# A gated feed-forward layer on one core: two x loads on one queue, gate pieces held on ScalarE, the first crossbar load in two

## The chip, the core and the metric

The kernel runs on one core of a Trainium2 chip. The core has TensorE (matrix multiply, "PE" in the profile; its weight loads are "PEld"), VectorE ("DVE"), ScalarE ("ACT"), GpSimd ("POOL") and SyncE ("SP"). [...] SyncE, ScalarE and GpSimd issue the DMA transfers between HBM and the on-chip memory. The metric is the device time of one launch in microseconds (us); lower is better. Before the change it is 163.2 us, the median of three runs (163.05 to 163.49).

## The reference

For 2048 rows of x with 640 columns the layer computes, in bf16:

```python
B, S, D, F = 1, 2048, 640, 1536

def reference(x, w_gate, w_up, w_down):
    g = _silu(x @ w_gate)
    u = x @ w_up
    return (g * u) @ w_down
```

`w_gate` and `w_up` are 640 x 1536, `w_down` is 1536 x 640.

## The kernel before, in words

The 2048 rows are worked in four blocks of 512 (`S_BLK`, the variable `sb`). The 640 columns of x are five slices of 128 (`KD`, `kd`), the 1536 columns in the middle twelve slices of 128 (`KF`, `fc`). A matmul contracts over the partitions, so x is needed turned: `xT` holds, for each `kd`, 128 features on the partitions and the rows along the free dimension. For each block and each `fc`, `proj` (line 197) makes five matmuls of `w_gate` into a psum buffer `pg` and five of `w_up` into `pu`; `gate` (line 212) takes silu of `pg` on ScalarE and multiplies it with `pu` on VectorE into `aT`. After the twelve `fc` of a block, `aT` is multiplied with `w_down` (lines 274 and 303) and stored. VectorE works out the last four rows of x separately by dot products (line 148) beside this.

Blocks 1 to 3 of x come through the crossbar: `turn_x` (line 108) issues a DMA that transposes on the way (line 110). The first block comes in two ways. Its first two chunks of 128 rows (`PE_X = 2`) are loaded plainly into `x_sb` (line 86), turned by TensorE with an identity matrix (line 190, five transposes for each chunk), and copied out of psum by ScalarE (`kd` 0 and 1) and VectorE (`kd` 2 to 4, line 195). Its last two chunks, the "late half", come through the crossbar.

The first loads and their queues stand in lines 112 to 122. x chunk 0 is on SyncE and x chunk 1 on ScalarE. The gate weights of the first two `fc` are cut at `kd` = 2 (`K_CUT`): pieces 0 and 1 on SyncE, pieces 2 to 4 on ScalarE. Those of the up weights: pieces 0 and 1 on GpSimd, 2 to 4 on SyncE. Then SyncE issues the crossbar's load for the late half, and after that the remaining weights in three larger chunks (line 83), `w_down` and the rest. ScalarE runs one small silu (line 122) so that its function table is loaded before it is needed. GpSimd builds the identity matrix with two instructions, a write of zeros and a select (`make_identity`, line 71).

`head` (line 221) writes out the order of the first two `fc` of the first block. TensorE begins with `N_WARM` small matmuls that compute nothing that is used (the fillers, line 177), then the ten transposes, then the gate matmuls of the early half (line 240: for `kd` 0 and 1 on 128 columns at a time, for `kd` 2 to 4 on 256), then the up matmuls of the early half, and then the late half: gate, up and `gate()` of `fc` 0, then the same for `fc` 1. `keep_order` fixes the order in which the instructions of TensorE, ScalarE and GpSimd were written; at the end of the body it does so for VectorE and SyncE. `issue_order` fixes the order of two instructions without a wait. The psum buffers `pg` and `pu` share four places, so that a later `fc` can only start when ScalarE or VectorE has read the buffer that it takes over.

Of the kernel before, what the change touches and what calls it, by code (L numbers as in the profile page):

```python
# [10 lines left out]
def _body(  # L11
# [8 lines left out]
    nc = tc.nc  # L20
# [3 lines left out]
    ACT = mybir.ActivationFunctionType  # L24
# [8 lines left out]
    KD = D // P  # L33
    KF = F // P
    S_BLK = 512
    NSB = S // S_BLK
    SUB = S_BLK // P
    DA = 512
    Q = 32
    N_WARM = 20  # L40
    T = 4
    WT_STEP = 4
    PE_X = 2
    K_CUT = 2
    ROW_J = 0
    W_CHUNKS = [(0, 2), (2, 4), (4, 8), (8, 12)]
    assert D % P == 0 and F % P == 0 and S % S_BLK == 0 and D > DA and SUB == 4
# [8 lines left out]
    ident = consts.tile([P, P], bf16)  # L56
    x_sb = consts.tile([P, PE_X, D], bf16)
    xT = consts.tile([P, KD, S], bf16)
    wg_sb = consts.tile([P, KD, F], bf16)
    wu_sb = consts.tile([P, KD, F], bf16)  # L60
# [7 lines left out]
    row_s = consts.tile([P, KF, T], f32)  # L68
    prod = consts.tile([P, D], f32)

    make_identity(nc, ident[:])

    x_v = x2.rearrange("(c p) d -> p c d", p=P)
    xt_v = x2.rearrange("s (kd p) -> s kd p", p=P)
    wg_v = w_gate.rearrange("(kd p) f -> p kd f", p=P)
    wu_v = w_up.rearrange("(kd p) f -> p kd f", p=P)
    wd_v = w_down.rearrange("(kf p) d -> p kf d", p=P)

    def wslice(a, b):
        return slice(a * P, b * P)  # L80
# [4 lines left out]
    def load_x(eng, c0, c1):  # L85
        eng.dma_start(out=x_sb[:, c0:c1, :], in_=x_v[:, c0:c1, :])

    def issue_order(a, b):
        tc.add_manual_dep(
            b,  # L90
            a.name,
            mybir.DependencyInfo(
                mybir.DependencyClass.NoSync, mybir.DependencyReason.DATA
            ),
            reason="issue_order",
        )

    def keep_order(engine):

        traced = [i for i in nc.cur_bb.bb.instructions if i.engine == engine]  # L100
        for a, b in zip(traced, traced[1:]):
            issue_order(a, b)

    ones = consts.tile([P, 1], bf16)
    silu_first = consts.tile([P, 1], f32)
    nc.vector.memset(ones[:], 1.0)  # L106

    def turn_x(c0, c1):
        s_sl = slice(c0 * P, c1 * P)
        nc.sync.dma_start_transpose(out=xT[:, :, s_sl], in_=xt_v[s_sl])  # L110

    load_x(nc.sync, 0, 1)
    load_x(nc.scalar, 1, 2)
    f_sl = wslice(*W_CHUNKS[0])
    for dst, src, first, second in (
        (wg_sb, wg_v, nc.sync, nc.scalar),
        (wu_sb, wu_v, nc.gpsimd, nc.sync),
    ):
        for eng, k_sl in ((first, slice(0, K_CUT)), (second, slice(K_CUT, KD))):
            eng.dma_start(out=dst[:, k_sl, f_sl], in_=src[:, k_sl, f_sl])  # L120
    turn_x(PE_X, SUB)
    nc.scalar.activation(silu_first[:], ones[:, 0:1], ACT.Silu)
    for a, b in W_CHUNKS[1:]:
        load_w(nc.sync, wg_sb, wg_v, a, b)
        load_w(nc.sync, wu_sb, wu_v, a, b)
# [4 lines left out]
    def turn_w(dst, src):  # L130
        for a in range(0, KF, WT_STEP):
            nc.sync.dma_start_transpose(
                out=dst[:, a : a + WT_STEP, :], in_=src[:, a : a + WT_STEP, :]
            )

    turn_x(1 * SUB, 2 * SUB)
    nc.sync.dma_start(
        out=x_row[:],
        in_=x2[S - T : S, :].rearrange("t d -> (t d)").partition_broadcast(P),
# [19 lines left out]
    def row_tail():  # L159
        for _ in dots:  # L160
            pass
        nc.scalar.activation(row_s[:], row_g[:], ACT.Silu)
        nc.vector.tensor_tensor(
            out=aT[:, :, S - T : S], in0=row_s[:], in1=row_u[:], op=ALU.mult
        )
# [3 lines left out]
    def do_dots(n):  # L169
        for _ in range(n):  # L170
            next(dots, None)
# [3 lines left out]
    def warm(n):  # L175
        for _ in range(n):
            nc.tensor.matmul(  # L177
                pw[:, 0:P],
                lhsT=ones[:].broadcast_to([P, P]),
                rhs=ones[:].broadcast_to([P, P]),  # L180
                start=True,
                stop=True,
            )

    def transpose_chunk(c, parts):
        c_sl = slice(c * P, (c + 1) * P)
        for copy, tag, k0, k1 in parts:
            pt = psum.tile([P, k1 - k0, P], bf16, tag=tag, name="pt")
            for kd in range(k0, k1):
                nc.tensor.transpose(  # L190
                    out=pt[:, kd - k0, :],
                    in_=x_sb[:, c, kd * P : (kd + 1) * P],
                    identity=ident[:],
                )
            copy(out=xT[:, k0:k1, c_sl], in_=pt[:])  # L195

    def proj(ps, w_sb, fc, sb, c0, c1):
        for kd in range(KD):
            nc.tensor.matmul(  # L199
                ps[:, c0:c1],  # L200
                lhsT=w_sb[:, kd, fc * P : (fc + 1) * P],
                rhs=xT[:, kd, sb * S_BLK + c0 : sb * S_BLK + c1],
                start=(kd == 0),
                stop=(kd == KD - 1),
            )

    def gu_tiles():
        pg = psum.tile([P, S_BLK], f32, tag="gu", name="pg", bufs=4)
        pu = psum.tile([P, S_BLK], f32, tag="gu", name="pu", bufs=4)
        return pg, pu  # L210

    def gate(pg, pu, sb, fc, n_s):

        s0 = sb * S_BLK
        sg = work.tile([P, S_BLK], f32, name="sg")
        nc.scalar.activation(sg[:, 0:n_s], pg[:, 0:n_s], ACT.Silu)  # L216
        nc.vector.tensor_tensor(  # L217
            out=aT[:, fc, s0 : s0 + n_s], in0=sg[:, 0:n_s], in1=pu[:, 0:n_s], op=ALU.mult
        )

    def head():

        dve, act = nc.vector.tensor_copy, nc.scalar.copy
        split = [(act, "po_a", 0, 2), (dve, "po_b", 2, KD)]
        late = PE_X * P
        (pg0, pu0), (pg1, pu1) = gu_tiles(), gu_tiles()  # L230
        warm(N_WARM)
        transpose_chunk(0, split)
        transpose_chunk(1, split)
        early = [(kd, c * P, (c + 1) * P) for c in range(PE_X) for kd in range(K_CUT)]
        early += [(kd, 0, late) for kd in range(K_CUT, KD)]
        for kd, c0, c1 in early:
            for fc, pg in ((0, pg0), (1, pg1)):


                nc.tensor.matmul(  # L240
                    pg[:, c0:c1],
                    lhsT=wg_sb[:, kd, wslice(fc, fc + 1)],
                    rhs=xT[:, kd, c0:c1],
                    start=(kd == 0 and c0 == 0),
                    stop=(kd == KD - 1),
                )
        proj(pu0, wu_sb, 0, 0, 0, late)
        proj(pu1, wu_sb, 1, 0, 0, late)
        for fc, pg, pu in ((0, pg0, pu0), (1, pg1, pu1)):
            proj(pg, wg_sb, fc, 0, late, S_BLK)  # L250
            proj(pu, wu_sb, fc, 0, late, S_BLK)
            gate(pg, pu, 0, fc, S_BLK)
        keep_order(mybir.EngineType.PE)
        keep_order(mybir.EngineType.Activation)
        keep_order(mybir.EngineType.Pool)

    head()
    for sb in range(NSB):
        n_s = S_BLK if sb < NSB - 1 else S_BLK - T
        for fc in range(KF):  # L260
            if sb == 0 and fc < 2:
                continue
            pg, pu = gu_tiles()
# [22 lines left out]
        for q in range(P // Q):  # L286
            nc.scalar.dma_start(
                out=out2[
                    sb * S_BLK : sb * S_BLK + n_t, DA + q * Q : DA + (q + 1) * Q
                ].rearrange("(i r) c -> r i c", r=Q),  # L290
                in_=ot_q[q * Q : (q + 1) * Q, :].rearrange("r (i c) -> r i c", c=Q),
            )

        for j in range(SUB):
# [5 lines left out]
            for c0, c1, tag in cols:  # L300
# [10 lines left out]
                if c1 < D:  # L311
                    nc.scalar.copy(ot[:], po[:])  # L312
                    eng = nc.sync
                else:
                    nc.vector.tensor_copy(out=ot[:], in_=po[:])  # L315
                    eng = nc.sync
                if 0 < j and not last:
                    do_dots(3)
                if sb == NSB - 1 and j == ROW_J:
                    row_tail()  # L320
                eng.dma_start(out=out2[s0 : s0 + P, c0:c1], in_=ot[:])
        if sb == 0:
            turn_x(2 * SUB, 3 * SUB)
            turn_w(wuT, wut_v)
            turn_x(3 * SUB, 4 * SUB)
# [72 lines left out]
def kernel(tc, *args):  # L398
    _body(tc, *args)
    tc.close()  # L400
    tc.compile()
    _trim(tc.nc)
# [30 lines left out]
```

## Time and profile before

| what | value |
|---|---|
| median of three runs | 163.2 us (163.05 to 163.49) |
| the profiled execution | 163.61 us, span 162.2 us |
| TensorE busy | 159.8 us, 98% of the span |
| VectorE busy | 110.8 us, 68% |
| ScalarE busy | 42.9 us, 26% |
| GpSimd busy | 1.5 us, 1% |
| DMA moved | 15.86 MB, mean 98 GB/s |

The span runs from the first to the last instruction of the profiled execution; its own time is 1.4 us longer. Busy time counts matmuls whose ends are modelled, so a busy TensorE is not a TensorE at its peak. The chain of waits follows the work that ended last back to the start, at each step to what released it; its shares say which engine or transfer the end hung on. A DMA's row on its issuer's queue shows the time in which the transfer is issued; the time from issue to landing is listed apart.

### The profile page before, as it was taken

Reading aid. Unit: us, or ns where it says so; the run is one execution under the profiler, and the core shown is the slowest. Engines: PE = TensorE matmul, PEld = TensorE weight load, DVE = VectorE, ACT = ScalarE, POOL = GpSimd, SP = SyncE. Lnnn points to the kernel's source line nnn. Section 1 sums busy time; section 2 is a strip of 40 time slices with the busy share of each in tenths; the row PEclk is TensorE's granted clock in tenths of the full one; section 3 lists DMA queues with packets and bytes.
Section 4 is the critical chain, followed back from the end, with each engine's and each line's share of the span. In section 5 each row is a group of like instructions: output and inputs, shape, how many; then the busy total and the mean of one; then the engine's idle time right before and its main releaser. Section 6 shows DMA issues by size and latency. Waiting matters only on the chain.

```text
span 162.2 us, 2119 instructions
## 1 busy us (share of the span) xinstructions
PE 159.8 (98%) x798; PEld 78.1 (48%) x798; DVE 110.8 (68%) x249; ACT 42.9 (26%) x74; POOL 1.5 (1%) x7
## 2 busy tenths in 40 slices
PE   8999999999999999999999999999999999999995
PEld 8854444444444444444444444444444444445454
DVE  1042233599469999979919999979964999993000
ACT  5132222112222222221222322221214222222121
POOL 3000000000000000000000000000000000000000
PEclk9999999999999999999999999999999999999999
DMA  7999999993179996003110000000320000000212
GB/s 215 275 343 350 363 217 220 240 216 87 35 164 161 205 177 136 4 0 34 65 65 0 0 4 2 0 0 1 63 68 33 0 0 0 0 0 4 50 39 73
DMA packets 42217, 15.86 MB, mean 98 GB/s; under 512 B 33216, under 2 KB 42048, under 8 KB 42208
## 3 DMA queue, kind: packets, MB, share of 16 engines
q1 hardware_dynamic: 33680, 14.75, 37.6%
q10 hardware_dynamic: 8480, 0.85, 3.4%
q8 instruction: 6, 0.10, 0.3%
q0 software_dynamic: 48, 0.13, 0.2%
q14 instruction: 3, 0.02, 0.1%
HBM read 6.88 MB, written 2.62 MB: 59 GB/s over the span
## 4 chain that ended last, share of the span: by engine, by line
PE 97%; DMA 2%; DVE 0%; issue 0%
PE pu L199 32%; PE pg L199 31%; PE po_a L303 26%; PE po_t L274 6%; DMA x_sb<-in_x_dram 2%; PE pg L240 1%; PE pt L190 1%; DVE ot_b L315 0%
## 5 line engine op out<-in xcount | busy, mean ns | idle before, releaser
L199 PE MATMUL pu<-xT,wu_sb 128*128 128x512 bf16 (+2 forms) x250 | 59.7, 370 | 0.0
L199 PE MATMUL pg<-xT,wg_sb 128*128 128x512 bf16 (+2 forms) x240 | 58.5, 374 | 0.0
L217 DVE TENSOR_TENSOR aT<-sg,pu 128x512 bf16<-128x512 f32 (+1 forms) x48 | 32.8, 684 | 32.4 <-PE pu L199 28.1
L216 ACT ACTIVATE sg<-pg 128x512 f32<-128x512 f32 (+1 forms) x48 | 28.6, 597 | 70.8 <-PE pg L199 66.2
L303 PE MATMUL po_a<-wd_sb,aT 128*128 128x512 bf16 (+2 forms) x216 | 42.8, 358 | 0.0
L148 DVE SCALAR_TENSOR_TENSOR prod<-wgT,x_row 128x640 f32<-128x640 bf16 x48 | 39.4, 821 | 1.1
L148 DVE SCALAR_TENSOR_TENSOR prod<-wuT,x_row 128x640 f32<-128x640 bf16 x48 | 39.4, 822 | 1.0
L199 PEld LDWEIGHTS <-wu_sb 128*128 128x128 bf16 x250 | 24.5, 98 | 27.3
L199 PEld LDWEIGHTS <-wg_sb 128*128 128x128 bf16 x240 | 23.5, 98 | 26.9
L303 PEld LDWEIGHTS <-aT 128*128 128x128 bf16 x216 | 20.7, 98 | 21.6
L312 ACT CAST ot<-po_a 128x512 bf16<-128x512 f32 (+1 forms) x17 | 9.5, 561 | 32.0 <-PE po_a L303 20.9
L274 PE MATMUL po_t<-aT,wd_sb 128*128 128x512 bf16 (+1 forms) x48 | 10.4, 366 | 0.0
L274 PEld LDWEIGHTS <-wd_sb 128*128 128x128 bf16 x48 | 4.7, 98 | 5.1
L315 DVE CAST ot_b<-po_a 128x128 bf16<-128x128 f32 x1 | 0.3, 292 | 9.9 <-PE po_a L303 9.9
L283 ACT CAST ot_t<-po_t 128x512 bf16<-128x512 f32 (+1 forms) x4 | 2.2, 559 | 11.6 <-PE po_t L274 11.6
L148 DVE DVE_READ_ACCUMULATOR prod<-wuT,x_row 128x1 f32 x48 | 4.0, 83 | 0.0
L148 DVE DVE_READ_ACCUMULATOR prod<-wgT,x_row 128x1 f32 x48 | 3.9, 82 | 0.0
L285 DVE STREAM_TRANSPOSE ot_q<-ot_t 128x512 bf16<-128x512 bf16 (+1 forms) x4 | 2.7, 678 | 1.7 <-ACT ot_t L283 1.7
L195 DVE COPY xT<-pt 128x384 bf16<-128x384 bf16 x2 | 0.7, 358 | 3.5 <-PE pt L190 3.5
L177 PE MATMUL pw<-ones 128*128 128x128 bf16 x20 | 2.3, 310 | 0.3 <-DVE ones L106 0.3
L240 PE MATMUL pg<-xT,wg_sb 128*128 128x128 bf16 (+1 forms) x14 | 2.2, 347 | 0.0
L177 PEld LDWEIGHTS <-ones 128*128 128x128 bf16 x20 | 2.0, 144 | 0.3 <-DVE ones L106 0.3
(16 smaller groups left out, 8.4 us busy)
## 6 DMA issues: line engine op xcount, KB each, us to landing
wd_sb<-in_w_down_dram SPq DMA_DIRECT2D x1, 1920.0 KB, 14.0
out_dram<-ot SPq DMA_DIRECT2D x15, 128.0 KB, 1.7
wg_sb<-in_w_gate_dram SPq DMA_DIRECT2D x2, 640.0 KB, 8.2
wu_sb<-in_w_up_dram SPq DMA_DIRECT2D x2, 640.0 KB, 8.8
x_row<-in_x_dram SPq DMA_DIRECT2D x1, 640.0 KB, 5.2
out_dram<-ot_q ACTq DMA_DIRECT2D x12, 32.0 KB, 1.9
wg_sb<-in_w_gate_dram SPq DMA_DIRECT2D x1, 320.0 KB, 4.4
wu_sb<-in_w_up_dram SPq DMA_DIRECT2D x1, 320.0 KB, 4.9
```

What stands on the lines that cost most here:

```text
L148: nc.vector.scalar_tensor_tensor(out=prod[:], in0=wT[:, fc, :], scalar=1.0, in1=x_row[:, t, :], op0=ALU.mult, op1=ALU.mult, accum_out=acc[ ...
L177: nc.tensor.matmul(pw[:, 0:P], lhsT=ones[:].broadcast_to([P, P]), rhs=ones[:].broadcast_to([P, P]), start=True, stop=True,)
L190: nc.tensor.transpose(out=pt[:, kd - k0, :], in_=x_sb[:, c, kd * P : (kd + 1) * P], identity=ident[:],)
L199: nc.tensor.matmul(ps[:, c0:c1], lhsT=w_sb[:, kd, fc * P : (fc + 1) * P], rhs=xT[:, kd, sb * S_BLK + c0 : sb * S_BLK + c1], start=(kd == 0 ...
L216: nc.scalar.activation(sg[:, 0:n_s], pg[:, 0:n_s], ACT.Silu)
L217: nc.vector.tensor_tensor(out=aT[:, fc, s0 : s0 + n_s], in0=sg[:, 0:n_s], in1=pu[:, 0:n_s], op=ALU.mult)
L240: nc.tensor.matmul(pg[:, c0:c1], lhsT=wg_sb[:, kd, wslice(fc, fc + 1)], rhs=xT[:, kd, c0:c1], start=(kd == 0 and c0 == 0), stop=(kd == KD ...
L274: nc.tensor.matmul(po_t[:], lhsT=wd_sb[:, kf, DA:D], rhs=aT[:, kf, sb * S_BLK : sb * S_BLK + n_t], start=(kf == 0), stop=(kf == KF - 1),)
L283: nc.scalar.copy(ot_t[:], po_t[:])
L285: nc.vector.transpose(out=ot_q[:], in_=ot_t[:])
L303: nc.tensor.matmul(po[:], lhsT=aT[:, kf, s0 : s0 + P], rhs=wd_sb[:, kf, c0:c1], start=(kf == 0), stop=(kf == KF - 1),)
L312: nc.scalar.copy(ot[:], po[:])
```

## The change

Both x chunks are loaded by SyncE. ScalarE first loads its function table with the small silu and then issues the gate pieces 0 and 1 and piece 2 of the up weights. The gate pieces write into `wg_sb`, into which GpSimd now writes one column (`wg_sb[:, 0, 0:1]`) between the two instructions of the identity matrix; so that transfer waits for this write. SyncE issues gate pieces 2 to 4 and up pieces 3 and 4. The identity's write of zeros is written out and `make_identity` is told to leave it away. The crossbar's load of the late half becomes two, for `kd` 0 to 2 and for `kd` 3 and 4 (`X_CUT = 3`), and the late half's matmuls are ordered so that those of `kd` 0 to 2 of three psum buffers come first; both `gate()` calls stand behind all of them. There are 19 fillers where there were 20.

On the queues this gives:

| queue | before | after |
|---|---|---|
| SyncE | x 0; gate 0-1; up 2-4; crossbar; weights | x 0; x 1; gate 2-4; up 3-4; crossbar 0-2; crossbar 3-4; weights |
| ScalarE | x 1; gate 2-4; table load, silu | table load, silu; gate 0-1 (waits for GpSimd's write); up 2 |
| GpSimd | zeros; select; up 0-1 | zeros; one column of `wg_sb`; select; up 0-1 |

```diff
--- before.py
+++ after.py
@@ -37,11 +37,12 @@
     SUB = S_BLK // P
     DA = 512
     Q = 32
-    N_WARM = 20
+    N_WARM = 19
     T = 4
     WT_STEP = 4
     PE_X = 2
     K_CUT = 2
+    X_CUT = 3
     ROW_J = 0
     W_CHUNKS = [(0, 2), (2, 4), (4, 8), (8, 12)]
     assert D % P == 0 and F % P == 0 and S % S_BLK == 0 and D > DA and SUB == 4
@@ -68,7 +69,9 @@
     row_s = consts.tile([P, KF, T], f32)
     prod = consts.tile([P, D], f32)
 
-    make_identity(nc, ident[:])
+    nc.gpsimd.memset(ident[:], 0.0)
+    nc.gpsimd.memset(wg_sb[:, 0, 0:1], 0.0)
+    make_identity(nc, ident[:], nomemset=True)
 
     x_v = x2.rearrange("(c p) d -> p c d", p=P)
     xt_v = x2.rearrange("s (kd p) -> s kd p", p=P)
@@ -105,21 +108,25 @@
     silu_first = consts.tile([P, 1], f32)
     nc.vector.memset(ones[:], 1.0)
 
-    def turn_x(c0, c1):
+    def turn_x(c0, c1, k0=0, k1=KD):
         s_sl = slice(c0 * P, c1 * P)
-        nc.sync.dma_start_transpose(out=xT[:, :, s_sl], in_=xt_v[s_sl])
-
+        nc.sync.dma_start_transpose(out=xT[:, k0:k1, s_sl], in_=xt_v[s_sl, k0:k1])
+
+    f_sl = wslice(*W_CHUNKS[0])
+
+    def load_k(eng, dst, src, a, b):
+        return eng.dma_start(out=dst[:, a:b, f_sl], in_=src[:, a:b, f_sl]).ins
+
+    nc.scalar.activation(silu_first[:], ones[:, 0:1], ACT.Silu)
     load_x(nc.sync, 0, 1)
-    load_x(nc.scalar, 1, 2)
-    f_sl = wslice(*W_CHUNKS[0])
-    for dst, src, first, second in (
-        (wg_sb, wg_v, nc.sync, nc.scalar),
-        (wu_sb, wu_v, nc.gpsimd, nc.sync),
-    ):
-        for eng, k_sl in ((first, slice(0, K_CUT)), (second, slice(K_CUT, KD))):
-            eng.dma_start(out=dst[:, k_sl, f_sl], in_=src[:, k_sl, f_sl])
-    turn_x(PE_X, SUB)
-    nc.scalar.activation(silu_first[:], ones[:, 0:1], ACT.Silu)
+    load_x(nc.sync, 1, 2)
+    gate_first = load_k(nc.scalar, wg_sb, wg_v, 0, K_CUT)
+    issue_order(gate_first, load_k(nc.sync, wg_sb, wg_v, K_CUT, KD))
+    load_k(nc.gpsimd, wu_sb, wu_v, 0, K_CUT)
+    load_k(nc.scalar, wu_sb, wu_v, K_CUT, K_CUT + 1)
+    load_k(nc.sync, wu_sb, wu_v, K_CUT + 1, KD)
+    turn_x(PE_X, SUB, 0, X_CUT)
+    turn_x(PE_X, SUB, X_CUT, KD)
     for a, b in W_CHUNKS[1:]:
         load_w(nc.sync, wg_sb, wg_v, a, b)
         load_w(nc.sync, wu_sb, wu_v, a, b)
@@ -194,8 +201,8 @@
                 )
             copy(out=xT[:, k0:k1, c_sl], in_=pt[:])
 
-    def proj(ps, w_sb, fc, sb, c0, c1):
-        for kd in range(KD):
+    def proj(ps, w_sb, fc, sb, c0, c1, k0=0, k1=KD):
+        for kd in range(k0, k1):
             nc.tensor.matmul(
                 ps[:, c0:c1],
                 lhsT=w_sb[:, kd, fc * P : (fc + 1) * P],
@@ -246,10 +253,18 @@
                 )
         proj(pu0, wu_sb, 0, 0, 0, late)
         proj(pu1, wu_sb, 1, 0, 0, late)
-        for fc, pg, pu in ((0, pg0, pu0), (1, pg1, pu1)):
-            proj(pg, wg_sb, fc, 0, late, S_BLK)
-            proj(pu, wu_sb, fc, 0, late, S_BLK)
-            gate(pg, pu, 0, fc, S_BLK)
+        for ps, w_sb, fc, k0, k1 in (
+            (pg0, wg_sb, 0, 0, X_CUT),
+            (pu0, wu_sb, 0, 0, X_CUT),
+            (pg1, wg_sb, 1, 0, X_CUT),
+            (pg0, wg_sb, 0, X_CUT, KD),
+            (pu0, wu_sb, 0, X_CUT, KD),
+            (pg1, wg_sb, 1, X_CUT, KD),
+            (pu1, wu_sb, 1, 0, KD),
+        ):
+            proj(ps, w_sb, fc, 0, late, S_BLK, k0, k1)
+        gate(pg0, pu0, 0, 0, S_BLK)
+        gate(pg1, pu1, 0, 1, S_BLK)
         keep_order(mybir.EngineType.PE)
         keep_order(mybir.EngineType.Activation)
         keep_order(mybir.EngineType.Pool)
```

## The prediction

> **What bounds the kernel now.** I read the chain of waits first, then the head of the run in order of time, then the windows and the DMA issues. The chain, from the page and with its pieces in order of time (start, length in us, what):
>
> ```profile
> PE 97%; DMA 2%; DVE 0%; issue 0%
> ...
> 0.00 2.77 DMA x_sb<-in_x_dram
> 2.77 0.05 issue
> 2.81 1.25 PE pt L190 x10
> 4.06 1.99 PE pg L240 x14
> 6.05 1.09 PE pu L199 x10
> 7.14 0.55 PE pg L199 x5
> ```
>
> From 2.81 us to the end TensorE never waits, so the change can move only two things: when TensorE begins real work, and whether some transfer comes too late behind it. The chain also shows that early work is dear. Line 240 streams 8 x 128 + 6 x 256 = 2560 columns in 1.99 us; the ten matmuls of line 199 right behind it also stream 10 x 256 = 2560 columns and take 1.09. So TensorE runs at about half rate until about 5.9 us. The column PEclk shows full clock there, so this is read from the columns, not from it.
>
> [...]
>
> The timeline of the head (start, length, engine, line):
>
> ```profile
> 0.00 0.39 SPq L86 DMA_DIRECT2D x_sb<-in_x_dram  x1
> 0.13 0.40 ACTq L86 DMA_DIRECT2D x_sb<-in_x_dram  x1
> ...
> 0.30 2.31 PE L177 MATMUL pw<-ones 128*128 128x128 bf16 x20 [0.30 <-DVE ones L106]
> ...
> 0.45 0.42 SPq L120 DMA_DIRECT2D wg_sb<-in_w_gate_dram  x1
> 0.56 0.45 ACTq L120 DMA_DIRECT2D wg_sb<-in_w_gate_dram  x1
> ...
> 1.04 1.28 ACT L122 ACT_TABLE_LOAD   x1 [1.04 <-issue]
> 1.42 1.86 SPq L110 DMA_TRANSPOSE xT<-in_x_dram  x1
> ...
> 2.81 1.25 PE L190 MATMUL pt<-ident,x_sb 128*128 128x128 bf16 x10 [0.20 <-DMA x_sb<-in_x_dram]
> ```
>
> The fillers end at 2.61 and TensorE then waits 0.20 us for x chunk 0. The DMA issues give the landings (issue to landing; add the start above):
>
> ```profile
> wg_sb<-in_w_gate_dram ACTq DMA_DIRECT2D x1, 192.0 KB, 3.7
> wu_sb<-in_w_up_dram SPq DMA_DIRECT2D x1, 192.0 KB, 4.5
> x_sb<-in_x_dram SPq DMA_DIRECT2D x1, 160.0 KB, 2.8
> x_sb<-in_x_dram ACTq DMA_DIRECT2D x1, 160.0 KB, 3.0
> wg_sb<-in_w_gate_dram SPq DMA_DIRECT2D x1, 128.0 KB, 3.2
> wu_sb<-in_w_up_dram POOLq DMA_DIRECT2D x1, 128.0 KB, 4.2
> ```
>
> Landed against first needed: x chunk 0 at 2.77, needed at once; x chunk 1 at 3.13, needed at 3.35 (five transposes, 0.107 us apart, behind 2.81); gate pieces 0-1 at 3.65, needed at 3.89 (ten transposes); gate pieces 2-4 at 4.3, needed at 4.75; up pieces at 5.2 and 5.4, needed near 5.9 and 6.1. The crossbar's half (L110, 5.0 us) lands at 6.4, needed at 6.98. All are slim, and all are edited.
>
> **The change, part by part.**
>
> *x chunk 0.* SyncE still issues it at 0.00. What changes is its company: chunk 1's packets on ScalarE's queue no longer run beside it; they stand behind it in SyncE's queue. Bounds for the landing: 2.80 if the 2.8 us are latency; 2.35 if what shares the engines sets its tail (in the windows the DMA share is 0.83 of the engines from 1 to 2 us and full from 2 to 3). Nothing excludes a small loss. I take 2.5, in the middle, since the engines are full when it finishes.
>
> [...]
>
> *19 fillers.* Twenty start from 0.30 to 2.31, so 0.106 us apart; one fewer ends them at 2.51 instead of 2.61. Worth up to 0.1 us if chunk 0 lands before 2.57, nothing otherwise.
>
> *x chunk 1.* SyncE's second slot is at 0.45 (gate pieces 0-1 have it now), 0.32 later than 0.13. By that slot's own row, 3.2 us, it lands at 3.65; by the x row of that queue, 2.8 us, at 3.25; if it follows chunk 0 without a gap, near 3.0. I take 3.15: its bytes had to wait for chunk 0's anyway. Then the second five transposes start at 3.2 and end at 3.7 (now 3.89).
>
> *Gate pieces 0-1.* They go to ScalarE behind the table load (1.28 us) and the first activation (0.20) in program order, and wait for GpSimd's new one-element write. GpSimd's small writes stand 0.03 to 0.04 us apart (0.31, 0.34, 0.38), so that write is done between 0.5 and 0.7. If ScalarE issues while the table loads, that is 0.65, and by the 3.0 us of its present first load the landing is 3.65, by SyncE's 3.2 it is 3.85. I take 3.7, just in time. Behind it on ScalarE stands only up piece 2 (near 1.1). The table load itself moves up from 1.04 to about 0.1; its user, the copy at 3.25, has always had it in time.
>
> *Gate pieces 2-4* move to SyncE's third slot, 0.91. Bounds: 4.3 by bytes ahead (x, x and gate pieces 0-1, as now), 5.4 by the present row of that slot (4.5 us). Needed at 3.7 + 8 x 0.107 = 4.56. I take 4.4, at no cost, because order and bytes ahead of it stay as they are; at 5.4 it would stall 0.85 us.
>
> *Up pieces.* GpSimd's two come 0.04 us later, 5.3; piece 2 on ScalarE and 3-4 on SyncE (near 1.4, now 0.91) have fewer bytes each and the same bytes ahead in sum: 5.4, bounds 5.0 to 5.9, needed at about 5.7 to 6.0. No cost taken.
>
> *The crossbar as two.* SyncE starts it one slot later, 1.85 instead of 1.42. A load of 512 columns issues in 3.17 us (median of L110), one of 256 in 1.86: so 0.55 fixed and 0.26 per block. Three blocks are 1.34, two 1.07, in sum 2.41: +0.55. The first part lands at 6.4 to 6.9, needed near 6.9; the second at 6.9 to 7.4, needed nine matmuls of 0.109 later, near 7.9. That is what the new order of TensorE covers; its instruction count is unchanged but for the filler.
>
> *SyncE's queue behind it* moves by 0.43 + 0.55 = 1.0 us at most. The next gate chunk (4.4 us from issue) lands by 8.75, now 7.8, needed at 9.05; the up chunk (4.9) by 9.85, now 8.85, needed at 10.1. Both are covered, by 0.3 and 0.25 us at worst; beyond that, lateness costs its full length. Later chunks have over 2 us.
>
> *Silu of the first block.* Its gate psum is complete 11 matmuls into the late half instead of 5, and ScalarE's 0.60 us ends near 2.0 us into that half; the next block reuses that buffer after 20 x 0.109 = 2.17 us. Covered by 0.15 us.
>
> **Sum.** First-layer work starts 0.15 to 0.25 us earlier (3.7, or 3.64 if chunk 1 is there by 3.05). If the rate doubles at the same moment as now, time gained in the slow stretch counts half: 0.1; if the moment moves along, whole: 0.25. I take 0.2. Against the profiled execution (span 162.2, 1.4 us around it, 163.61 in all) that is 163.4. That execution is 0.4 above the median of 163.2, so on the median's scale the forecast is 163.0.
>
> **Rivals.**
>
> 1. *Slower: ScalarE does not issue past its table load.* For: on GpSimd the DMA starts at 1.02, only after the select ended at 0.95. Against: that DMA is made by GpSimd itself, and no row shows ScalarE holding a DMA behind work. Then gate pieces 0-1 go out at about 1.6 and land at 4.6 (3.0 us) to 5.3 (3.7): TensorE waits 0.9 to 1.6 us in the slow stretch. If the doubling keeps its moment, that costs 0.45 to 0.8; if idleness delays it, all. 163.6 to 164.6. It decides once the pieces land later than 3.89.
>
> [...]
>
> 2. *Faster by more: the doubling comes earlier.* Without the pause of 0.2 us TensorE is busy from 0.30 on. If unbroken work sets the moment, it comes 0.4 to 1 us sooner than 5.9, worth 0.2 to 0.5 beside the 0.2: 162.3 to 162.7. For: the slow stretch ends only 3.1 us behind that pause. Against: one trace cannot tie the two.
>
> 3. *Nothing moves.* Chunk 0 still lands at 2.77 and the slack elsewhere holds: 163.2. For: 2.8 us for an uncrowded first load may be plain latency.
>
> 4. *Slower: chunk 1 or gate pieces 2-4 late* (3.65, 5.4): 0.3 to 0.85 us of pause, counted half to whole: 163.3 to 164.0.
>
> **How the numbers follow.** Forecast 0.37, rival 1 0.17, rival 2 0.24, rival 3 0.12, rival 4 0.10. Faster or slower means by over 0.3% (0.49 us: below 162.71 or above 163.69), about what a measurement of this kernel can tell from no change. Faster: rival 2 and 0.06 of the forecast's tail, 0.30. Slower: 0.16 of rival 1 and 0.08 of rival 4, 0.24. Same: 0.46. The range runs from 162.4, inside rival 2, to 164.0, which leaves out the upper half of rival 1; the forecast's own range is 162.7 to 163.2.
>
> **What would show it.** x chunk 0's DMA piece at the head of the chain 2.5 instead of 2.77; ScalarE's DMA start near 0.65, inside the table load (at 1.6, rival 1 holds); line 247 of the new kernel beginning near 3.7 (3.85 to 3.89 now); no DMA behind it in the chain. If the columns of line 247 take much less than 1.99 us, rival 2 holds. A releaser on wg_sb or on the crossbar's xT among TensorE's waits would make me wrong upward.

## The result, and the profile after

The changed kernel takes 165.07 us (median of 13 runs, 163.82 to 166.60) against 163.49 us before (13 runs, 163.05 to 163.98). The ratio is 1.0092, 95% interval 1.0070 to 1.0113: about 0.9% slower, and its runs are spread over 2.8 us where those of before lie within 0.9. The ratios here and below leave out runs over 1.5% above the fastest of the same kernel (166.60 us here, and one run each of three experiments: 167.25, 165.62 and 167.15), so a kernel whose times scatter can look better by its ratio than by its median. The profiled execution has 166.27 us, span 164.9, near the top of the 13 runs, so its waits show the mechanism rather than the typical size.

The head of the changed kernel in order of time (start, length, engine, line):

```profile
0.00 0.87 SPq L89 DMA_DIRECT2D x_sb<-in_x_dram  x2
0.12 1.28 ACT L120 ACT_TABLE_LOAD   x1
...
0.66 0.45 ACTq L118 DMA_DIRECT2D wg_sb<-in_w_gate_dram  x1
...
0.91 0.43 SPq L118 DMA_DIRECT2D wg_sb<-in_w_gate_dram  x1
...
2.31 1.27 PE L197 MATMUL pt<-ident,x_sb 128*128 128x128 bf16 x10
...
5.43 0.62 PE L247 MATMUL pg<-xT,wg_sb 128*128 128x128 bf16 x8 [1.84 <-DMA wg_sb<-in_w_gate_dram]
...
6.23 0.83 PE L247 MATMUL pg<-xT,wg_sb 128*128 128x256 bf16 x6 [0.18 <-DMA wg_sb<-in_w_gate_dram]
```

TensorE begins its transposes at 2.31 us instead of 2.81, without a wait: the x loads come earlier than in the execution profiled before. But then it stands idle for 1.84 and 0.18 us, both times for gate weights. The DMA issues of the same stretch (from issue to landing, to be added to the starts above):

```profile
x_sb<-in_x_dram SPq DMA_DIRECT2D x2, 160.0 KB, 2.3
...
wg_sb<-in_w_gate_dram SPq DMA_DIRECT2D x1, 192.0 KB, 5.3
wg_sb<-in_w_gate_dram ACTq DMA_DIRECT2D x1, 128.0 KB, 4.7
```

The x loads land 2.3 us after their issue, where they took 2.8 and 3.0. Gate pieces 0-1 land at 0.66 + 4.7 = 5.4 us (3.65 before), pieces 2-4 at 0.91 + 5.3 = 6.2 (4.3 before). The chain of waits of the changed kernel, in order of time:

```profile
0.91 5.27 DMA wg_sb<-in_w_gate_dram
6.18 0.05 issue
6.23 0.83 PE pg L247 x6
7.06 2.11 PE pu L206 x10
9.17 0.64 PE pg L206 x3
9.81 0.64 PE pu L206 x3
10.45 0.57 PE pg L206 x5
11.02 0.22 PE pu L206 x2
11.23 0.22 PE pg L206 x2
11.45 0.55 PE pu L206 x5
```

The ten up matmuls of the early half begin at 7.06 us instead of 6.05: the wait, less what the earlier start and the now fast gate matmuls give back, is 1.01 us. But these ten then take 2.11 us instead of 1.09, and the late half behind them takes 2.83 us (9.17 to 12.00) instead of 2.19 (7.14 to 9.33). Together 1.01 + 1.02 + 0.64 = 2.67 us, which is the whole difference of the two spans (164.9 - 162.2). More than half of it is not wait but matmuls at half rate. The windows of the changed kernel show it (stretch, length, busy time of each engine, granted TensorE clock, DMA share, GB/s):

```profile
5.40:6.90 1.50, 1.29 (x15) 1.06 (x16) 0.00 (x0) 0.00 (x0) 0.00 (x0) 1.00 0.65 129
7.00:8.00 1.00, 1.00 (x7) 0.69 (x5) 0.00 (x0) 0.00 (x0) 0.00 (x0) 0.50 1.19 283
9.00:10.00 1.00, 1.00 (x6) 0.70 (x5) 0.00 (x0) 0.00 (x0) 0.00 (x0) 0.50 1.14 317
10.40:11.40 1.00, 1.00 (x12) 0.88 (x9) 0.00 (x0) 0.35 (x1) 0.00 (x0) 1.00 1.10 347
```

TensorE is at full clock when the gate weights arrive at 5.43 us, and falls to half 1.5 us later, 0.7 us behind the second wait. Windows set around the two edges (0.69 from 6.8 to 7.2, 0.92 from 10.3 to 10.7) put the half-rate stretch at 6.95 to 10.37, 3.4 us.

Between 3.59 us and the drop at 6.95 TensorE had been idle for 2.02 us (1.84 and 0.18). How much idle time such a drop takes is not shown.

One caution about the early part. The column shows 1.00 from the first microsecond on, also where the matmuls stream at half rate. The moment at which the rate doubles is read from the starts of the matmuls, 0.107 us apart for 128 columns at half rate and 0.054 to 0.056 at full. It differs widely between executions: 5.8 us in the kernel before, between 3.3 and 5.4 in the changed one; and in four executions of experiments below, in which TensorE had until then paused for 0.2 us at most, 3.0, 4.0, 5.4 and 6.1.

### The profile page after: what moved, and what is told of

It is laid out like the page before. It is cut to its first block, busy times and chain, and to the rows that moved or that the text cites. A ratio compares the mean times of both kernels' runs of the same rounds, so it can differ in the third digit from the quotient of the medians.

```text
span 164.9 us, 2120 instructions
## 1 busy us (share of the span) xinstructions
PE 160.6 (97%) x797; PEld 78.1 (47%) x797; DVE 110.7 (67%) x249; ACT 42.8 (26%) x74; POOL 1.5 (1%) x8
## 4 chain that ended last, share of the span: by engine, by line
PE 95%; DMA 3%; SPq 0%; DVE 0%; issue 0%
PE pu L206 32%; PE pg L206 31%; PE po_a L318 26%; PE po_t L289 6%; DMA wg_sb<-in_w_gate_dram 3%; PE pg L247 1%; SPq L89 0%; DVE ot_b L330 0%
## 5 line engine op out<-in xcount | busy, mean ns | idle before, releaser
L206 PE MATMUL pu<-xT,wu_sb 128*128 128x512 bf16 (+2 forms) x250 | 61.3, 377 | 0.0
L206 PEld LDWEIGHTS <-wu_sb 128*128 128x128 bf16 x250 | 25.0, 100 | 27.8
L206 PEld LDWEIGHTS <-wg_sb 128*128 128x128 bf16 x240 | 23.7, 99 | 27.2
L247 PE MATMUL pg<-xT,wg_sb 128*128 128x128 bf16 (+1 forms) x14 | 1.5, 244 | 2.0 <-DMA wg_sb<-in_w_gate_dram 2.0
L247 PEld LDWEIGHTS <-wg_sb 128*128 128x128 bf16 x14 | 1.0, 98 | 2.5 <-DMA wg_sb<-in_w_gate_dram 2.5
```

Of the source, the lines that this page charges most:

```text
L206: nc.tensor.matmul(ps[:, c0:c1], lhsT=w_sb[:, kd, fc * P : (fc + 1) * P], rhs=xT[:, kd, sb * S_BLK + c0 : sb * S_BLK + c1], start=(kd == 0 ...
L247: nc.tensor.matmul(pg[:, c0:c1], lhsT=wg_sb[:, kd, wslice(fc, fc + 1)], rhs=xT[:, kd, c0:c1], start=(kd == 0 and c0 == 0), stop=(kd == KD ...
```

## The experiments

Theory A: the gate pieces come late by their new place, TensorE idles, and the idleness sets the clock back. Its rival, theory B: the two crossbar loads and the later weight chunks cost the time. The first runs separate the change's parts.

**The queues alone.** The changed kernel with the late half, the crossbar load and the fillers as before:

```diff
-    N_WARM = 19
+    N_WARM = 20
-    turn_x(PE_X, SUB, 0, X_CUT)
-    turn_x(PE_X, SUB, X_CUT, KD)
+    turn_x(PE_X, SUB)
...
+        for fc, pg, pu in ((0, pg0, pu0), (1, pg1, pu1)):
+            proj(pg, wg_sb, fc, 0, late, S_BLK)
+            proj(pu, wu_sb, fc, 0, late, S_BLK)
+            gate(pg, pu, 0, fc, S_BLK)
```

> Only the change's queues: both x on SyncE, gate pieces 0-1 and up piece 2 on ScalarE behind GpSimd's write; one crossbar load, the old order of the late half, 20 fillers. Theory A (the gate pieces come late by their new place, TensorE stands idle before line 247's matmuls, and an idle stretch sets the clock back): the whole loss is here, 1.2 to 2.0 us above the kernel before, and TensorE waits 0.5 us or more for the gate weights. Theory B (the loss comes from the two crossbar loads and the later weight chunks): within 0.4 us of the kernel before.

165.73 us (4 runs) against 163.55; ratio 1.0109 (1.0049 to 1.0169). In its profiled execution TensorE waits 0.99 and 0.65 us for gate weights. The whole loss is in the queues, as theory A has it.

**The rest alone.** The changed kernel with the first loads on their old queues:

```diff
-    nc.gpsimd.memset(wg_sb[:, 0, 0:1], 0.0)
...
     load_x(nc.sync, 0, 1)
-    load_x(nc.sync, 1, 2)
...
+    load_x(nc.scalar, 1, 2)
+    load_k(nc.sync, wg_sb, wg_v, 0, K_CUT)
+    load_k(nc.scalar, wg_sb, wg_v, K_CUT, KD)
     load_k(nc.gpsimd, wu_sb, wu_v, 0, K_CUT)
+    load_k(nc.sync, wu_sb, wu_v, K_CUT, KD)
...
+    nc.scalar.activation(silu_first[:], ones[:, 0:1], ACT.Silu)
```

> Only the rest of the change: two crossbar loads, the new order of the late half, 19 fillers; the first loads on the queues of the kernel before. Theory A: within 0.4 us of the kernel before, no wait of TensorE behind the first transpose. Theory B: 1 us or more above it.

163.27 us (10 runs) against 163.55, ratio 0.9988 (0.9976 to 0.9999). Theory B falls. Timed a second time:

> The kernel of the earlier run with only the two crossbar loads, the new order of the late half and 19 fillers, timed again: 0.0 to 0.4 us below the kernel before. If it is not below, the rest of the change is worth nothing on its own.

163.22 us against 163.27, ratio 0.9998 (0.9985 to 1.0011). The split crossbar load, the new order and the missing filler cost nothing, and what they may gain is not clear of nothing.

**Without the hold.**

```diff
-    nc.gpsimd.memset(wg_sb[:, 0, 0:1], 0.0)
```

> The changed kernel without GpSimd's one-element write, so that ScalarE issues gate pieces 0-1 at about 0.1 us instead of 0.66. Theory A1 (the hold makes the pieces late): they land before 3.5 us, TensorE does not wait for them, and the time is 162.7 to 163.5 us. Theory A2 (two x loads in one queue ahead of all weights are the cause, with or without the hold; gate pieces 2-4 in SyncE's third slot come late): still 0.8 us or more above the kernel before, with the wait now on gate pieces 2-4.

163.64 us (10 runs; nine lie between 163.00 and 163.93, one at 165.62), ratio 1.0002 (0.9982 to 1.0022). ScalarE issues at 0.25 us, and pieces 0-1 land at 2.9, ahead of x chunk 1, for which TensorE now waits 0.34 us. A1 holds for the landing, but not the gain that it foresaw: the kernel is no faster than before. Later, at 9.16 us, TensorE also waits 0.17 us for the silu of the first block. The change without the hold is neutral.

**More fillers in the wait.**

```diff
         transpose_chunk(1, split)
+        warm(10)
```

> The changed kernel with ten more fillers behind the transposes, before line 247's first matmul; TensorE is busy for about 1.05 us more of the wait, and the transfers are as in the changed kernel. If the clock that is set back after the idle stretch carries a good part of the loss: faster than the changed kernel by 0.4 us or more in the median, with fewer runs above 165.5 us. If the loss is the wait alone: equal to the changed kernel, or up to 0.3 us slower where the pieces land early.

164.24 us, ratio 1.0083 (1.0046 to 1.0120) where the changed kernel has 1.0092. The median is 0.8 us below the changed kernel's and 2 of 10 runs are above 165.5 us where 5 of 13 were. That is what was expected if the clock carries a good part of the loss; but the two ratios do not differ beyond their intervals, so this run alone does not price the clock. The next pair does.

**The price of an idle stretch.** The kernel before, with a matmul behind the transposes that waits for the crossbar's load and whose result is not used; once with TensorE idle until then, once with 28 fillers ahead of it (the line with `warm` stands in the second alone).

```diff
         transpose_chunk(1, split)
+        warm(28)
+        nc.tensor.matmul(
+            pw[:, 0:P],
+            lhsT=xT[:, 0, late : late + P],
+            rhs=ones[:].broadcast_to([P, P]),
+            start=True,
+            stop=True,
+        )
```

> The kernel before with one more matmul (result unused) behind the ten transposes, which waits for the crossbar's load (6.4 us): TensorE stands idle from about 3.9 to 6.4, then waits for nothing. It prices an idle stretch. If idleness costs only its own time: the same as the next run, within 0.3 us. If it also sets the clock back: 0.5 us or more slower than the next run, with the columns of the first matmuls behind it at half rate in the profile or some time later.

> The same wait, with 28 more fillers between the transposes and it, so that TensorE is busy until about 6 us. 2.5 us of delay, of which the half-rate stretch up to about 5.8 us gives back up to 1 us: 1.3 to 2.2 us above the kernel before.

Idle: 167.60 us (4 runs), ratio 1.0252 (1.0204 to 1.0299). Filled: 165.65 (4 runs), ratio 1.0121 (1.0086 to 1.0156). The wait for the same load costs 2.0 us more in the median when TensorE idles through it. The chain of waits of the idle one, in order of time:

```profile
6.59 0.29 PE pw L234
6.88 2.13 PE pg L247 x14
9.01 1.56 PE pu L199 x10
10.57 0.55 PE pg L199 x5
```

and of the filled one:

```profile
6.92 0.23 PE pw L235
7.15 1.10 PE pg L248 x14
8.25 1.09 PE pu L199 x10
9.35 0.55 PE pg L199 x5
```

Fourteen gate matmuls take 2.13 us behind the idle stretch and 1.10 behind the filled one; with the ten up matmuls (1.56 against 1.09) that is 1.5 us. These two executions differ by 1.2 us, as the load landed 0.3 us earlier in the idle one. The idle stretch of 3.16 us is paid twice here: once as a wait, once as half-rate work behind it. The windows of the idle one show half clock from 6.4 us, just before work resumed, to 9.85: again 3.4 us (its mean granted clock over the span of 165.6 us is 0.99).

The traces of other experiments seem to show a second form of the same price. Where the rate had not yet doubled when the pause came, it doubled late: at 8.7 us with all first loads but GpSimd's on SyncE, at 11.3 with the longer hold, at 11.5 with the queues alone, against 5.4 to 6.3 in the executions with the old queues in which TensorE had no long pause. And a wait of 1.4 us (GpSimd's load on SyncE) cost nothing behind it in the one execution profiled. So the same pause has a different price from one execution to the next, which fits the spread of the changed kernel's times; no run separates that from the spread of the landings.

**Why the gate pieces come late.** The remaining runs vary where and when the first loads are issued. Their results stand in one table behind them.

The hold a little shorter, its write put ahead of the identity's zeros:

```diff
+    nc.gpsimd.memset(wg_sb[:, 0, 0:1], 0.0)
     nc.gpsimd.memset(ident[:], 0.0)
-    nc.gpsimd.memset(wg_sb[:, 0, 0:1], 0.0)
```

> The changed kernel with GpSimd's one-element write put ahead of the identity's write of zeros, so that ScalarE issues gate pieces 0-1 at about 0.5 us: 0.13 us earlier than in the changed kernel, but still behind the issue of x chunk 1 (0.45), which is ahead of it in the changed kernel and behind it in the run without the hold. Theory C1 (what counts is whether the pieces are issued ahead of x chunk 1): the last part of pieces 0-1 still lands at 4.2 us or later, time 0.8 us or more above the kernel before. Theory C2 (each tenth of a us of hold counts): they land near 3.6 us, time within 0.5 us of the kernel before.

The hold longer, its write behind the select:

```diff
-    nc.gpsimd.memset(wg_sb[:, 0, 0:1], 0.0)
     make_identity(nc, ident[:], nomemset=True)
+    nc.gpsimd.memset(wg_sb[:, 0, 0:1], 0.0)
```

> The changed kernel with GpSimd's one-element write behind the select, so that ScalarE issues pieces 0-1 at about 1.0 us, behind SyncE's gate pieces 2-4. A longer hold: pieces 0-1 land at 4.5 us or later, and the time is 1.5 us above the kernel before or more. If the hold does not matter beyond 0.66 us: as the changed kernel, 0.8 to 1.6 us above.

GpSimd's transfer moved to SyncE:

```diff
-    load_k(nc.gpsimd, wu_sb, wu_v, 0, K_CUT)
...
+    load_k(nc.sync, wu_sb, wu_v, 0, K_CUT)
     load_k(nc.sync, wu_sb, wu_v, K_CUT + 1, KD)
```

> The changed kernel with up pieces 0-1 issued by SyncE, between gate pieces 2-4 and up pieces 3-4, instead of by GpSimd. If GpSimd's transfer, whose packets stand between the gate weights', makes some of the 16 parts late: gate pieces 0-1 land before 3.9 us and 2-4 before 4.8, and the time falls by 0.8 us or more from the changed kernel's. If not: pieces 0-1 still land after 4.2 us and the time stays 0.8 to 2.2 us above the kernel before.

The two gate transfers exchanged:

```diff
-    nc.gpsimd.memset(wg_sb[:, 0, 0:1], 0.0)
+    nc.gpsimd.memset(wg_sb[:, K_CUT, 0:1], 0.0)
...
-    gate_first = load_k(nc.scalar, wg_sb, wg_v, 0, K_CUT)
-    issue_order(gate_first, load_k(nc.sync, wg_sb, wg_v, K_CUT, KD))
+    gate_second = load_k(nc.scalar, wg_sb, wg_v, K_CUT, KD)
+    load_k(nc.sync, wg_sb, wg_v, 0, K_CUT)
```

> The changed kernel with the two gate transfers exchanged: pieces 0-1 on SyncE behind the two x loads (about 0.9 us), pieces 2-4 on ScalarE behind GpSimd's write (0.66 us). Again two queues with gate weights side by side. Theory D: pieces 0-1 land at 4 us or later, and the time stays 0.8 us or more above the kernel before. If only ScalarE's queue makes pieces late: pieces 0-1 land by 3.7 us and pieces 2-4 at 5 us or later.

Everything but GpSimd's transfer on SyncE, without a hold, and then GpSimd's too:

```diff
-    nc.gpsimd.memset(wg_sb[:, 0, 0:1], 0.0)
...
-    gate_first = load_k(nc.scalar, wg_sb, wg_v, 0, K_CUT)
-    issue_order(gate_first, load_k(nc.sync, wg_sb, wg_v, K_CUT, KD))
-    load_k(nc.gpsimd, wu_sb, wu_v, 0, K_CUT)
-    load_k(nc.scalar, wu_sb, wu_v, K_CUT, K_CUT + 1)
-    load_k(nc.sync, wu_sb, wu_v, K_CUT + 1, KD)
+    load_k(nc.sync, wg_sb, wg_v, 0, K_CUT)
+    load_k(nc.sync, wg_sb, wg_v, K_CUT, KD)
+    load_k(nc.gpsimd, wu_sb, wu_v, 0, K_CUT)
+    load_k(nc.sync, wu_sb, wu_v, K_CUT, KD)
```

> The changed kernel with all first loads but GpSimd's on SyncE, in the order x 0, x 1, gate pieces 0-1, gate pieces 2-4, up pieces 2-4, crossbar; ScalarE issues nothing and nothing is held. Pieces 0-1 are issued at about 0.9 us, 0.25 us later than in the changed kernel, but no other queue moves anything beside them. Theory D (they come late because two queues share the engines and the gate pieces of both advance side by side): they land by 3.8 us, and TensorE waits under 0.5 us for them. Theory E (they come late because they are issued late): they land at 4.3 us or later, as in the changed kernel, and the time is no better than the changed kernel's.

```diff
-    load_k(nc.gpsimd, wu_sb, wu_v, 0, K_CUT)
+    load_k(nc.sync, wu_sb, wu_v, 0, K_CUT)
```

> The kernel with all first loads on SyncE, now GpSimd's too (up pieces 0-1 behind gate pieces 2-4): one queue, nothing beside it. If GpSimd's packets made the last parts of gate pieces 0-1 late in the earlier run (5.0 us): they land by 3.6 us, and the time falls by 0.5 us or more. If a late part comes about without any other queue: 4.3 us or later again, and the time as in the earlier run, 0.5 to 1.3 us above the kernel before.

The kernel before, x chunk 1 on ScalarE as there, with only the gate transfers held:

```diff
-    make_identity(nc, ident[:])
+    nc.gpsimd.memset(ident[:], 0.0)
+    nc.gpsimd.memset(wg_sb[:, 0, 0:1], 0.0)
+    nc.gpsimd.memset(wg_sb[:, K_CUT, 0:1], 0.0)
+    make_identity(nc, ident[:], nomemset=True)
```

> The kernel before, x chunk 0 on SyncE and chunk 1 on ScalarE as there, but both gate transfers wait for a one-element write of GpSimd each, so that pieces 0-1 (SyncE) and 2-4 (ScalarE) are issued at about 0.66 us instead of 0.45 and 0.56. Theory F1 (a gate transfer issued after about 0.6 us comes late, wherever the x loads stand): the engines move under 250 GB/s from 2.25 to 3.25 us, pieces 0-1 land after 3.9 us, and the time is 0.8 us or more above the kernel before. Theory F2 (it takes both x loads in one queue ahead of the gate weights): over 280 GB/s there, pieces 0-1 by 3.9 us, time within 0.5 us of the kernel before.

All in one table. "Issued" and "landed" are gate pieces 0-1, "GB/s" is what the DMA engines moved from 2.25 to 3.25 us, "wait" is what TensorE waited for gate weights, all from the one profiled execution of each. "Profiled" is the time of that execution, with the range of all the kernel's runs; the ratio is over the compared runs.

| kernel | x loads on | issued | landed | GB/s | wait | profiled | ratio to before (95%) |
|---|---|---|---|---|---|---|---|
| before | SyncE, ScalarE | 0.45 | 3.65 | 303 | 0 | 163.61 (163.05 to 163.98) | |
| queues of before, rest changed | SyncE, ScalarE | 0.46 | 3.5 | 311 | 0 | 163.33 (162.92 to 163.72) | 0.9988 (0.9976 to 0.9999) |
| before, gate held | SyncE, ScalarE | 0.65 | 3.85 | 292 | 0.16 | 163.88 (163.39 to 164.33) | 1.0016 (1.0000 to 1.0032) |
| no hold | SyncE | 0.25 | 2.9 | 316 | 0 | 163.93 (163.00 to 165.62) | 1.0002 (0.9982 to 1.0022) |
| short hold | SyncE | 0.51 | 3.9 | 260 | 0 | 163.71 (163.22 to 165.01) | 1.0008 (0.9983 to 1.0033) |
| changed | SyncE | 0.66 | 5.4 | 176 | 2.0 | 166.27 (163.82 to 166.60) | 1.0092 (1.0070 to 1.0113) |
| changed, more fillers | SyncE | 0.65 | 4.5 | 220 | 0.3 | 163.92 (163.92 to 166.33) | 1.0083 (1.0046 to 1.0120) |
| long hold | SyncE | 1.02 | 5.5 | 123 | 2.0 | 167.25 (165.60 to 167.25) | 1.0181 (1.0150 to 1.0213) |
| GpSimd's load on SyncE | SyncE | 0.64 | 4.9 | 159 | 1.4 | 163.96 (163.77 to 165.87) | 1.0063 (1.0024 to 1.0101) |
| gate pieces exchanged | SyncE | 0.91 | 5.9 | 124 | 2.4 | 166.50 (164.26 to 167.15) | 1.0102 (1.0063 to 1.0141) |
| all but GpSimd's on SyncE | SyncE | 0.91 | 5.0 | 188 | 1.5 | 165.68 (163.95 to 165.68) | 1.0081 (1.0043 to 1.0119) |
| all on SyncE | SyncE | 0.91 | 4.2 | 145 | 0.7 | 163.90 (163.90 to 165.30) | 1.0055 (1.0032 to 1.0078) |

Landings of two rows compare fairly only where the profiled executions stand alike in their ranges: the changed kernel's stands near the top of its range, those with more fillers and with all loads on SyncE are the lowest of theirs.

The column GB/s is read from windows like these, of the kernel before:

```profile
2.25:3.25 1.00, 0.81 (x9) 0.54 (x7) 0.00 (x0) 0.28 (x3) 0.00 (x0) 1.00 1.00 303
```

of the changed kernel:

```profile
2.25:3.25 1.00, 1.00 (x12) 0.95 (x11) 0.16 (x1) 0.37 (x1) 0.00 (x0) 1.00 0.62 176
```

and of the kernel before with only the gate transfers held:

```profile
2.25:3.25 1.00, 1.00 (x12) 0.88 (x11) 0.03 (x1) 0.74 (x3) 0.00 (x0) 1.00 1.08 292
```

The second number from the right is the DMA engines' busy share. In the changed kernel the engines are only 0.62 busy just when the gate pieces should move: the x loads landed at 2.3 and 2.7, and of the gate pieces' 16 parts the first landed at 3.0. In the other rows with both x loads on SyncE and the gate pieces issued after 0.6 us the share lies between 0.53 and 1.03. The rate does not set the landing by itself: at 145 GB/s the pieces landed at 4.2, at 188 GB/s at 5.0.

What follows. In this arrangement of the queues the hold decides: 0.25, 0.51, 0.66 and 1.02 us of issue give ratios of 1.0002, 1.0008, 1.0092 and 1.0181. C1 falls. C2 holds in time, though the pieces landed at 3.9, not near 3.6, and the price does not grow evenly. At 0.51 the wait is elsewhere, for x chunk 1, which landed at 3.6 there; in that run:

```profile
3.67 0.71 PE L197 MATMUL pt<-ident,x_sb 128*128 128x128 bf16 x5 [0.62 <-DMA x_sb<-in_x_dram]
```

But the same lateness costs only 0.16% when x chunk 1 stays on ScalarE (292 GB/s, pieces at 3.85): F1 falls, F2 holds, and it takes both, the late issue and the x loads in one queue. That comparison is not quite clean, since pieces 2-4 go out at 0.69 there and at 0.91 in the changed kernel, and the other loads are those of the kernel before.

GpSimd's transfer on its own is not the cause (4.9 us without it in its old place). Exchanging the gate pieces made those on SyncE as late (5.9), so ScalarE's queue is not the cause either, as theory D said. But D fails where the gate pieces share one queue: it asked for 3.8 us, they landed at 5.0, and the ratio of 1.0081 is no better than the changed kernel's within the intervals, as theory E said. That test was not clean, as GpSimd's load still ran beside them. With it in the same queue too they landed at 4.2, between the two expected outcomes (3.6, or 4.3 and later). That is the lowest of ten runs set against the highest of five, and the ratios (1.0055 and 1.0081) overlap, so whether a neighbour in another queue costs anything is not shown.

What stays open is why some of the 16 parts in which a transfer lands come so much later than the others. In the trace of the changed kernel half of the parts of pieces 0-1 had landed at 3.8 us and all but one at 4.1; the last came at 5.4. Had it come with the one before it, TensorE would have waited about 0.6 us instead of 1.84 (an estimate: 4.11 us, less the 3.59 at which it stood idle, and 0.05 from landing to start). Nor is it a matter of bytes: from 5.5 to 6.0 us, with one part of pieces 2-4 still missing, the engines moved 20 GB/s. In the run with all but GpSimd's load on SyncE, 12 of 16 had landed by 3.24, the last at 5.0. In the kernel before, the last part is within 0.5 us of the middle one. In the changed kernel TensorE started at 5.43, 0.05 us behind the last part (5.38).

## Why the prediction was wrong

The forecast lay 0.2 us below the kernel before; the changed kernel came out 0.9% above it, 1.5 us on the same scale. Two steps failed, the landing of the gate pieces and the price of an idle stretch.

- *x chunk 0* was taken to land at 2.5 and *chunk 1* at 3.15; the transposes show both earlier, by 2.3 and 2.8. But the 2.77 us of before was a late one: in five other executions with the old queues chunk 0 landed at 2.2 to 2.5 and chunk 1 at 2.75 to 2.95, so the gain from the queue is nearer 0.2 us than 0.5, and the rest of the 0.5 is the luck of the execution profiled before. The ranges, 2.2 to 2.35 against 2.2 to 2.8, overlap, so they do not decide whether the queue gains anything. That the earlier start shortens the kernel, the 0.2 us of the sum, no run shows: without the hold the ratio is 1.0002.
- *ScalarE issues during its table load*: right, at 0.66 inside 0.12 to 1.40. Rival 1 did not occur. What it foresaw behind it did, the pieces landing past 4.6 us and TensorE waiting, at a price somewhat too low (163.6 to 164.6 us).
- *Gate pieces 0-1* are the first step that failed: "I take 3.7, just in time", between 3.65 and 3.85. They landed at 5.4. The bounds came from adding the old rows' time from issue to landing to a new issue time. Those rows belonged to transfers with another place in the queues: the same hold with x chunk 1 on ScalarE landed at 3.85, with both x loads on SyncE at 5.4, with the engines 0.62 busy in between and the last of the 16 parts 1.6 us behind the middle one. Why that part came so late stays open.
- *Gate pieces 2-4*: "at no cost, because order and bytes ahead of it stay as they are". They landed at 6.2, beyond even the upper bound of 5.4. The bytes ahead did stay; the landing is not set by bytes alone. From 2.25 to 3.25 us the rate fell from 303 to 176 GB/s, which at 300 GB/s is worth about 0.4 us (an estimate from these two figures); the rest came with the last parts: 14 of the 16 had landed by 4.43.
- *Counting early time half to whole* is the second step that failed. An idle stretch was taken to cost at most its length; the idle and filled pair shows 2.0 us on top in the medians, and in its two profiles 1.5 us more for the matmuls behind the stretch. In the changed kernel's profile, with the clock at 0.50 from 6.95 to 10.37 us, it is the 2.11 us for ten matmuls that took 1.09, and 0.64 us more in the late half.
- *The crossbar, the later weight chunks, the silu, the order of the late half and the fillers* were taken at no cost: right, 0.9988 and 0.9998 for all of them together; only in the run without the hold did TensorE wait for the silu (0.17 us). SyncE's next chunk went out at 4.56 us, 1.2 later than before (taken: 1.0), and stayed covered.
- *Rival 4* had the mechanism for pieces 2-4 (late, TensorE pauses) at a chance of 0.10 and 163.3 to 164.0 us. The place was right; both the lateness and the price of the pause were too small. *Rival 2*, an earlier doubling, seems to appear (the gate matmuls on line 247 run at full rate from 5.43), but its condition does not: with TensorE busy from 0.3 us and no pause over 0.2 us the doubling came at 3.0, 4.0, 5.4 and 6.1 in four executions. So unbroken work does not set the moment, and here the gain was lost again behind the wait.

## What to carry to other kernels

A time from issue to landing belongs to the queue and the moment in which it was measured: for gate pieces 0-1 it was 3.2 us in the kernel before, 2.6 without the hold and 4.7 in the changed kernel. When a load is moved, look at what keeps the DMA engines busy between the loads before it and its own first packets (from 2.25 to 3.25 us their share was 1.00 in the kernel before and 0.62 in the changed one), not only at the bytes ahead. A load that is just in time should be priced with the clock in mind: a pause of some 2 us in the first matmuls cost nearly as much again in half-rate work behind it (1.7 us in the changed kernel's trace). In the idle and filled pair, fillers through the wait saved 2.0 us (167.60 against 165.65); ten of them in the changed kernel's wait showed no clear gain (1.0083 against 1.0092). Holding a load back for another's sake has an edge: 0.15 us less hold was the difference between no loss and 0.9%. And one profiled execution shows one draw: when the rate doubles and when a load lands both vary between executions by more than what a small change is worth (the doubling from 3.0 to 6.1 us, x chunk 0 on the old queues from 2.2 to 2.8, where the forecast gain was 0.2), so times from issue to landing are best taken from several.

## What the runs showed that was not expected

- With both x loads in one queue and the gate pieces issued after 0.6 us, the DMA engines stood at 0.53 to 0.68 busy from 2.25 to 3.25 us in five of the kernels above, in the middle of the first loads.
- In the changed kernel the clock fell to half only after work had resumed, and stayed there for 3.4 us of full work (6.95 to 10.37 us); in the idle run it fell just before work resumed, and also for 3.4 us.
- The moment at which the rate doubles lay between 3.0 and 6.1 us in four executions with hardly a pause from 0.3 us on.
- In the changed kernel the last of the 16 parts of gate pieces 0-1 landed 1.6 us behind the middle one (5.4 against 3.8), which no sum over bytes shows.
